# A gated linear attention and a spatial gating network on one core: weight loads on ScalarE's queue, with a new table of the order of all work

## The chip, the cores and the metric

One core of a Trainium2 chip. The metric is the device time of one execution in microseconds (us), lower is better. Engines: PE (TensorE, matmuls; PEld are its weight loads), DVE (VectorE), ACT (ScalarE), POOL (GpSimd), SP (SyncE, which here only requests DMA transfers).

## The reference

Two stages. The first is a recurrence over 768 time steps, for 4 batches and 8 heads of size 48; the second a network with a spatial gate on its result.

```python
# stage 1: q, k, v, alpha: (4, 8, 768, 48)
for t in range(S):
    state = alpha[:, :, t, :, None] * state + np.einsum('bhd,bhe->bhde', k[:, :, t], v[:, :, t])
    y[:, :, t] = np.einsum('bhd,bhde->bhe', q[:, :, t], state)
x = y.transpose(0, 2, 1, 3).reshape(B, S, H * D)             # (4, 768, 384)
# stage 2
h = np.maximum(x @ w_in, 0.0)                                # w_in (384, 1024)
u, v = h[..., :512], h[..., 512:]
v_n = (v - mean(v)) / np.sqrt(var(v) + 1e-06)                # over the last axis
v_s = np.einsum('ts,bsd->btd', w_spatial, v_n) + b_spatial   # w_spatial (768, 768)
return (u * v_s) @ w_out                                     # w_out (512, 384)
```

## The kernel before

The sequence is cut into chunks of 128 steps, six to a batch, 24 in all (numbered i). The recurrence within a chunk becomes matmuls with cumulative sums of log alpha. Chunks 0 to 7 are handled as four pairs (PAIRS, j = 0 to 3): one load of 384 KB per tensor brings 256 steps, two neighbouring steps to a partition, which are then split by parity (`par`). The other 16 chunks are loaded one by one (192 KB each).

**Steps of a pair** (function `pair`; the single chunks in `first` have the same ones without the final p): `lnp` takes the log of alpha on ACT (tile la); `cump` sums it with triangular matrices (le_pair, lt_pair) on PE; `einvp` and `eexpp` exponentiate on ACT; `ktp` and `qtp` scale k and q (tiles kt, qt; ktp on POOL or DVE, qtp on DVE); `vbp` casts v (POOL or ACT); `tr` transposes kt and qt on PE; `ev` copies the transposes out of PSUM (tile kqT, on ACT or DVE); `sc` forms scores on PE, and `m` masks them on DVE (tile ptm, masks mask2 and mask4); `updq` forms the chunk's contribution to the state; `z`, `S`, `sb` (DVE, POOL, POOL or DVE) bring the state forward and write it to the tile sbd; `ya` and `y` form the output on PE; `xs` copies it out, `xt` transposes it, `xe` copies it to xT.

**Steps of the second stage**, by batch b: `v.b.t` and `u.b.f.th` are the two halves of x @ w_in, evacuated with relu; `bn`, `rs`, `vn` normalise v; `s` multiplies by w_spatial (transposed once by `wt`, copied by `we`), and DVE adds the bias while it copies the result to a buffer vsb (the bias comes in by the matmuls `bb` and their copies `be` into bsp_bc); `g` multiplies by u (tile gT; POOL, in the last batch DVE too); `o` multiplies by w_out, and ACT copies the result out for the store `st`.

**Weights.** `fetch` loads six pieces of 768 KB: w_in in two halves (w_in.1 is for v, w_in.0 for u), w_spatial in three, w_out. A piece lands in one of two buffers raw_w and is cast from there (operations `cast`) to bf16 on POOL, ACT or DVE; a piece's request waits until the casts of the piece two before it are done. All requests, of q, k, v, alpha, of the weights and of the output's stores, are made by SP; only the small bias is requested by POOL.

**Order.** Nothing is scheduled when the kernel is built: each step is an `Op` with the engines that it may run on, and `PLAN` is a table written out in the code, which names every operation in the order of emission, with a letter for its engine (P, D, A, G for POOL, S for SP's request, Q for the landing). Each engine executes its operations in this order, and waits at each for its inputs. Numbers behind a colon are columns of filler: `bank` then first issues matmuls of the constant tile `junk` (128x128 fp32, set by a memset on DVE) on the bank that the operation is about to use. PE executes them whether or not the operation's inputs are there. Before has such fillers at ten places, 3,572 columns in all, 1,216 of them ahead of the first `cump`.

```python
for cols in fill:
    n = cols // 4
    nc.tensor.matmul(out=flat[:, 0:cols]..., lhsT=junk, rhs=junk[:, None, 0:n].to_broadcast([128, 4, n]), ...)
```

**Constants.** The operation `consts` emits memsets on DVE and triangles on POOL in one go, `junk` first; `cz` 0, 1 and 2 emit the rest (second buffers' padding, sbd, ones_row and eps; mask4 and ut_ones).

Of the kernel before, what the change touches and what calls it, by code (L numbers as in the profile page):

```python
# [36 lines left out]
class Slot:  # L37
# [5 lines left out]
    "kt": {"POOL": 0.9},  # L43
    "vb": {"POOL": 0.48, "ACT": 0.42},
# [6 lines left out]
    "o": {"ACT": 0.4},  # L51
# [6 lines left out]
S34 Q35 S36 Q37 G32 G0 Q33 S38 Q39 S94 Q95 S40 Q41 A42 P53:512:512:192 A54 D1 D2 D56 P43 S96 Q97 S98 Q99 S100 Q101  # L58
S163 Q164 S4 Q5 S165 Q166 S167 Q168 P59:464 G58 G48 A44 A45 A55 D46 D57 D47 P249:304 P49 P61 A50 P51 D52 D60 A62 A102
A250 P71:304 P74 P113 P103 D72 D73 D76 D75 P63 P77:172 D65 A114 D116 P119:148 A104 A64 A115 A105 A78 G66 G67 G106 D107  # L60
D117 D68 P79 P81 P111 P121 P247 P109 G3 G69 A108 A82 A80 D120 D122 D112 D110 P83 A84 A171 D248 S169 Q170 S9 Q10 S307
Q308 P131 P134 D133 D136 D132 D135 G70 G118 P172:228 P182 P123:240 A183 A8 A173 A124 P137 P138 A139 A174 G7 G6 D125
P85 G126 D128 D185 G127 G129 G175 P88 P142 P140 A86 A184 D176 D186 A143 A89 P188 P190 P180 P144 P178 A141 A191 A145
A181 P146 G11 G12 S309 Q310 S311 Q312 D130 D87 D179 D90 D189 P157 A187 A177 A158 A147 A13 P197 P200 P192 D199 D201
D198 D194 D202 P151:196 P155 A315 A193 A91 P326 P316 A327 P203 P153 P204 G195 G196 G329 A317 A328 A318 P149 A205 A154
D159 D156 D152 D330 G319 P208 P334 A209 P206 D320 P332 P324 P210 P322 D92 D335 D325 D333 D148 A207 P212 A211 A150 P347
P215 P221 A213 A160 A222 A216 S14 Q15 P223 P227 S18 Q19 D93 D323 D161 D348 D349 D214 G16 G17 A224 A228 P225 P229 A226
A21 P232 A234 D231 D230 D233 G20 P235:300 P238 S313 Q314 G331 G321 P344 P336 S367 Q368 S369 Q370 S22 Q23 S371 Q372
A237 A236 D217 D162 D346 A240 D338 A239 A218 D219 D220 A375 A337 P251 P263 P259 P376 A377 A378 G339 P264 D345 D341
D265 P260 D261 P255 P252 A380 A25 A24 D381 D253 P256 D257 G340 G342 G379 S409 Q410 S373 Q374 S446 Q447 S411 Q412 S413  # L70
Q414 S415 Q416 S26 Q27 S480 Q481 S448 Q449 S482 Q483 S450 Q451 S484 Q485 P383 A385 A417 S452 Q453 S577 Q578 S486 Q487
S581 Q582 S579 Q580 S583 Q584 P244 P241 P350 A246 D384 D245 D242 D243 P390 P354 P418 D392 D391 A351 A355 G262 G343
A420 A382 G254 G266 P279 P352 P271 P356 P393 P272 A353 A357 A419 G421 A422 A394 P280 P361 P386 P275 P395 A362 A424
A396 A31 D273 D423 D281 D387 P425 D397 D427 D426 D363 G282 G388 P276 P358 D277 P398 G258 G389 G278 G30 A399 A454 A359
A28 A488 P405 P432 P267 P455 P401 A402 A457 A456 D29 P291 P489 P268 A490 A459 D406 D433 D400 D434 D360 P283 P428 D269
D460 A492 D429 D493 G458 G491 P435 A284 A292 A436 G274 G461 G270 G430 G431 S648 Q649 S617 Q618 S650 Q651 S611 Q612
S652 Q653 S613 Q614 S690 Q691 S615 Q616 S694 Q695 S654 Q655 S692 Q693 P287 P462 P437 P495 P403 D463 D464 D497 D496
A288 A439 A438 P440 A585 A441 A364 D404 P469 P498 P295 P465 P586 P303 D471 D470 D466 D500 D499 A296 A587 A588 A590
A304 P299 G494 G467 G468 G589 G592 D591 D442 P472 A473 P501 P407 P474 A502 A300 P503 P593 P596 A443 A505 A408 D475
D476 P477 A478 D504 D366 D594 D595 D445 D444 D597 D365 P506 P600 P515 D601 D516 A507 A479 A508 D509 D602 A656 A510  # L80
A619 P517 P525 P513 P519 P529 P657 P533 P620 D511 D512 P526 P530 A514 A659 A658 A621 A661 A622 A698 A624 D518 D520
D527 D531 D662 P545 P534 P699 A701 A700 A703 D625 G598 G599 G660 G626 G623 G528 D535 P546 D547 P630 P627 P664 P537
# [12 lines left out]
D808 D906 D804 G805 G880 G809 G983 D985 D943 P822 P884 P811 D812 A885 P823 P908 P886 P945 D824 P814 P911 P815 D912
D909 D816 G813 G817 G913 G825 A910 A887 A888 A947 A946 P889 A1016 A890 P952 P915 P987 D953 D916 D954 P830 P1017 P831
P818 A988 A1019 A1050 A1018 D917 P948 P819 P1051 D949 A1021 A986 A989 D1022 D832 G950 P834 A1052 G951 G1020 P990 P842
P918 A835 A1054 D820 D991 D1055 A843 A919 P838 P1024 P994 P920 D1025 D921 D995 D996 A839 A1023 G914 G833 G1053 G992
S1048 Q1049 S575 Q576 S836 Q837 S844 Q845 S293 Q294 S289 Q290 S571 Q572 S305 Q306 S301 Q302 S555 Q556 A922 A1026 S297
Q298 S285 Q286 S840 Q841 P826 P955 P827 D828 A956 P1057 P957 P1031 D958 P1027 D1028 D1033 D1032 P997 P923 A1058 A1059  # L100
A959 P969 P1060 A1056 A998 P999 D1062 D1001 D1061 D970 G821 G829 G993 G1029 A1000 A924 P960 P846 P1034 A961 A847 G1030
P1063 A1035 A1064 P1002 P963 P1036 P1065 D925 D891 A1003 D962 D1066 P850 P967 A1067 A1037 D1004 A926 D928 P1068 A964
A1038 P1039 D927 D968 A851 A1005 A1069 A1040 D1006 D1041 D1007 D1070 P965 P854 P1076 P1080 P1078 P1074 D966 A1079 A855
A1071 A1081 D1075 D1072 D1073 D1077 P1094 P1082 P1106 P1086 P1083 P1098 P1095 P1090 P1102 P1087 P1107 P1091 P1103
P1110 P1099 P1111 D1096 D1084 G1085 D1088 D1097 D1108 D1092 D1093 G1089 P1113 D1104 G1109 G1105 D1112 D1100 D1101
P1117 P1121 S852 Q853 S563 Q564 S856 Q857 S848 Q849 A1114 S1115 Q1116 A1118 P1133 S1119 Q1120 A1122 P1125 A1134 S1123
Q1124 P1129 S1135 Q1136 A1126 P1137 S1127 Q1128 A1130 A1138 S1131 Q1132 S1139 Q1140
# [16 lines left out]
def kernel(  # L124
# [113 lines left out]
    def constants(_):  # L238

        nc.vector.memset(junk, 0.5)  # L240
        nc.gpsimd.memset(le_pair, 0.0)
        nc.vector.memset(mask2[:, 0].bitcast(FP32), 0.0)
        zero_padding(lap_bufs[0])
# [4 lines left out]
        nc.vector.memset(lt_pair.bitcast(FP32), 0.0)  # L248
        for t, base in ((le_pair, 0), (lt_pair, 1)):
            nc.gpsimd.affine_select(  # L250
                out=t, in_=t, compare_op=ALU.is_gt, fill=1.0, base=base, channel_multiplier=1,
                pattern=[[-1, 128]],
            )
            nc.gpsimd.memset(t[0:64, 64:128], 0.0)
        for t in (ktp_bufs[0], qtp_bufs[0]):
            zero_padding(t)
        make_identity(nc, ident)
        nc.vector.memset(mask2[:, 1].bitcast(FP32), 0.0)
        for par in range(2):
            for ci in range(2):  # L260
                rows = slice(64 * ci, 64 * ci + 64)
                nc.gpsimd.affine_select(
                    out=mask2[rows, par], in_=mask2[rows, par], compare_op=ALU.is_gt, fill=1.0,
                    base=par, channel_multiplier=2, pattern=[[0, 4], [-1, 2], [-2, 64]],
                )
# [891 lines left out]
```

## Time and profile before

| what | value |
|---|---|
| median of 3 runs | 143.13 us (143.12 to 143.7) |
| profiled execution, its own time | 143.08 us |
| its span in the profile | 141.3 us |
| clock granted to PE | 1.00 of full speed |
| DMA | 28.64 MB, mean 203 GB/s |
| first matmul of the second stage (v.0.0) | starts at 20.23 us |
| last matmuls end | about 138 us |

The span runs from the first to the last recorded activity; the time of an execution is 1.8 us longer. A line of the profile names the line of the code, the engine, the operation, the written tile, `<-` the read tiles, and the shape. In the views in order of time the first two columns are the start and the duration in us; in square brackets stands how long the engine had been idle and what ended that. Where several neighbouring instructions are merged, `x4` is their number. Durations of matmuls include some 0.17 us of a modelled tail, so the distance between two starts tells more than a duration. A request's line (SPq) shows how long the request held its engine, not the transfer.

### The profile page before, as it was taken

How to read it: one execution, taken by the hardware profiler on the slowest of the kernel's cores; microseconds unless marked ns; L12 is line 12 of the kernel's file. 1: busy time of each engine (PE TensorE's matmuls, PEld its weight loads, DVE VectorE, ACT ScalarE, POOL GpSimd, SP SyncE). 2: the span in 40 equal slices, each digit the busy share in tenths (PEclk: the TensorE clock that was granted, in tenths of full speed). 3: DMA queues.
4: the chain of work that ended last, by engine and by line, in shares of the span. 5: the costliest groups of instructions: out<-in, count | busy, mean ns of one | idle time of the engine just before them, and what ended most of it. 6: DMA issues, size and time to landing. Idle time of an engine off the chain costs nothing.

```text
span 141.3 us, 4968 instructions
## 1 busy us (share of the span) xinstructions
PE 133.2 (94%) x1912; PEld 84.2 (60%) x1923; DVE 118.3 (84%) x291; ACT 108.6 (77%) x282; POOL 83.4 (59%) x146
## 2 busy tenths in 40 slices
PE   7989798999999999999999999999999989999990
PEld 3457575575667656565675665656666656566560
DVE  7479878999989599999998898989979779894940
ACT  3677569988989969889887999997889969940061
POOL 6722986293449596982299899500799993000720
PEclk9999999999999999999999999999999999999999
DMA  4999999999898989989799999979978690112044
GB/s 102 323 323 332 331 272 311 225 320 238 241 232 156 283 161 208 205 161 212 154 205 179 193 217 177 222 143 195 250 151 203 225 375 24 70 56 102 0 164 170
DMA packets 89000, 28.64 MB, mean 203 GB/s; under 512 B 83728, under 2 KB 87440, under 8 KB 88976
## 3 DMA queue, kind: packets, MB, share of 16 engines
q1 hardware_dynamic: 88944, 28.32, 81.6%
q8 instruction: 15, 0.25, 0.7%
q14 instruction: 9, 0.07, 0.2%
q0 software_dynamic: 32, 0.00, 0.0%
HBM read 23.60 MB, written 4.72 MB: 200 GB/s over the span
## 4 chain that ended last, share of the span: by engine, by line
PE 71%; DVE 9%; POOL 7%; issue 5%; ACT 4%; ACTq 0%; POOLq 0%; DVEq 0%
PE bank L828 47%; PE bank L187 4%; DVE ptm L594 3%; PE bank L719 2%; PE bank L754 2%; POOL sbd L199 2%; POOL gT L989 2%; PE bank L511 2%; PE bank L782 2%; DVE ptm L765 2%; PE bank L740 1%; PE bank L583 1%; POOL kt L690 1%; PE bank L666 1%; DVE kqT L199 1%
## 5 line engine op out<-in xcount | busy, mean ns | idle before, releaser
L828 PE MATMUL bank<-w_spT,vn 128*128 128x384 bf16 x192 | 36.8, 326 | 0.0
L989 POOL TENSOR_TENSOR gT<-vsb,uT 128x384 bf16<-128x384 f32 x28 | 25.7, 923 | 14.9 <-DVE vsb L976 14.4
L690 POOL TENSOR_TENSOR kt<-kc,binv 128x384 bf16<-128x384 f32 x16 | 14.6, 914 | 13.4 <-ACT bc L685 8.6
L765 DVE TENSOR_TENSOR ptm<-bank,mask 128x512 bf16<-128x512 f32 x32 | 20.7, 682 | 1.9 <-PE bank L398 1.2
L828 PEld LDWEIGHTS <-vn 128*128 128x128 bf16 x192 | 16.6, 97 | 9.5 <-issue 0.2
L976 DVE TENSOR_TENSOR vsb<-bank,bsp_bc 128x384 f32<-128x384 f32 x31 | 16.5, 551 | 4.2 <-PE bank L828 2.5
L828 PE MATMUL bank<-xT,w_in 128*128 128x384 bf16 x96 | 18.7, 326 | 0.0
L828 PE MATMUL bank<-w_out_sb,gT 128*128 128x384 bf16 (+1 forms) x100 | 18.7, 319 | 0.0
L828 PE MATMUL bank<-w_in,xT 128*128 128x512 bf16 x61 | 17.2, 379 | 0.8 <-issue 0.2
L344 POOL TENSOR_TENSOR state<-state,bc 128x192 f32<-128x192 f32 x20 | 10.4, 520 | 11.4 <-DVE state L337 5.4
L197 ACT COPY kqT<-bank 128x512 bf16<-128x512 bf16 x21 | 12.1, 599 | 3.9 <-PE bank L719 1.1
L199 POOL CAST sbd<-state 64x192 bf16<-64x192 f32 x38 | 13.3, 350 | 2.0
L893 DVE BATCH_NORM_STATS2 stats<-v_sb 128x6 f32<-128x512 bf16 x20 | 13.7, 683 | 0.3 <-ACT v_sb L203 0.3
L203 ACT ACTIVATE v_sb<-bank 128x512 bf16<-128x512 f32 x20 | 11.8, 605 | 1.4 <-PE bank L828 1.3
L197 ACT CAST x_sb<-bank 128x384 bf16<-128x384 f32 x24 | 11.4, 490 | 1.5 <-PE bank L623 1.3
L828 PEld LDWEIGHTS <-w_in 128*128 128x128 bf16 x96 | 8.8, 97 | 5.9
L828 PEld LDWEIGHTS <-gT 128*128 128x128 bf16 x100 | 8.9, 97 | 5.6 <-DVE gT L989 0.4
L199 DVE COPY kqT<-bank 128x512 bf16<-128x512 bf16 x27 | 10.5, 416 | 1.9 <-PE bank L511 1.0
L187 PE MATMUL bank<-junk 128*128 128x512 f32 (+9 forms) x24 | 10.2, 529 | 1.1 <-DVE junk L240 1.1
L594 DVE TENSOR_TENSOR ptm<-bank,mask 128x512 bf16<-128x512 f32 x16 | 10.2, 683 | 0.5 <-PE bank L583 0.4
L197 ACT COPY xT<-bank 128x192 bf16<-128x192 bf16 (+1 forms) x26 | 9.4, 379 | 1.6 <-PE bank L398 1.1
L197 ACT COPY o_sb<-bank 128x384 f32<-128x384 f32 x9 | 4.4, 484 | 8.0 <-PE bank L828 8.0
(126 smaller groups left out, 284.0 us busy)
## 6 DMA issues: line engine op xcount, KB each, us to landing
ac<-in_alpha_dram SPq DMA_DIRECT2D x16, 192.0 KB, 4.1
kc<-in_k_dram SPq DMA_DIRECT2D x16, 192.0 KB, 4.8
qc<-in_q_dram SPq DMA_DIRECT2D x16, 192.0 KB, 4.1
vc<-in_v_dram SPq DMA_DIRECT2D x16, 192.0 KB, 3.8
raw_w<-in_moe_w_spatial_dram SPq DMA_DIRECT2D x3, 768.0 KB, 6.8
out_dram<-raw_w SPq DMA_DIRECT2D x11, 192.0 KB, 2.5
out_dram<-o_sb SPq DMA_DIRECT2D x9, 192.0 KB, 1.8
ac<-in_alpha_dram SPq DMA_DIRECT2D x4, 384.0 KB, 5.0
```

The source lines that it names most:

```text
L187: nc.tensor.matmul(out=flat[:, 0:cols].rearrange("p (a b) -> p a b", a=4), lhsT=junk, rhs=junk[:, None, 0:n].to_broadcast([128, 4, n]), st ...
L197: nc.scalar.copy(out=out, in_=in_)
L199: ENG[eng].tensor_copy(out=out, in_=in_)
L203: nc.scalar.activation(out=out, in_=in_, func=AF.Relu)
L344: ENG[eng].tensor_tensor(out=st["state"], in0=st["state"], in1=st["bc"][:, :, None].to_broadcast([128, HP, D]), op=ALU.mult)
L594: nc.vector.tensor_tensor(out=st[f"ptm{par}"][:, s], in0=st[f"pt{s}{par}"], in1=mask2[:, par], op=ALU.mult)
L690: ENG[eng].tensor_mul(out=k_blocks(kt3)[:, :, :, 0:D], in0=quad(st["kc"]), in1=st["binv"])
L765: nc.vector.tensor_tensor(out=st["ptm"][:, s], in0=st[f"pt{s}"], in1=mask4, op=ALU.mult)
L828: return lambda ps: nc.tensor.matmul(out=out(ps), lhsT=lhsT(), rhs=rhs(), start=start, stop=stop)
L893: nc.vector.bn_stats(out=stats, in_=d["v_sb"][:, tt, :])
L976: nc.vector.tensor_tensor(out=hold["vs"], in0=ps[:, 0:TH], in1=bsp_bc[:, th, :], op=ALU.add)
L989: ENG[eng].tensor_tensor(out=bt[b]["gT"][:, dsl, cols], in0=hold["vs"], in1=bt[b]["uT"][:, dsl, cols], op=ALU.mult)
```

## The change

Four things change.

1. The six weight pieces are requested by ACT on its own queue (`nc.scalar.dma_start`) in place of SP.
2. `PLAN` is replaced as a whole. PE has the same operations; the order on all engines, the engines of many operations, and the fillers are new: 6,060 columns at six places. 1,216 go ahead of the first bias matmul `bb` (now the first operation of PE, in front of `cump.0`), 916 ahead of `cump.1`, 1,260 and 1,024 ahead of the first transposes, 632 ahead of `tr.q.1.0`, 1,012 ahead of `updq.0`, and none later. SP now requests alpha of pairs 0 and 1 first, then k and q of both, then v of both.
3. The engines that some operations may use are widened: kt, vb, vbp, o, xs, and g in every batch may go to DVE too. By the tables this moves to DVE: 5 more g (8 in all, 3 before), 3 kt, 5 vb, 3 o, half of the last o, 4 xs, 8 xe, a bias copy and a cast of w_in; from DVE: 10 u and 8 ev to ACT, 2 ktp and one sb to POOL.
4. The constants are single operations (`c_junk`, `c_la`, `c_kt`, ...), each with its place in the table, and each step waits for those it reads. On DVE the order becomes la, ones_col, mask2[0], sbd, qt (second buffer), ones_row and eps, mask2[1], kt, la (second), halves_of with lt_pair, junk, qt, and further on the second kt. On POOL it becomes the bias request, one half of mask2, ident, the triangles, the other half of mask2.

Besides, the bias of the last `s` group is added by ident and bsp_bc in place of ones_row and b_sp_sb.

```diff
 ENGINES = {
-    "kt": {"POOL": 0.9},
-    "vb": {"POOL": 0.48, "ACT": 0.42},
+    "kt": {"POOL": 0.9, "DVE": 0.47},
+    "vb": {"POOL": 0.48, "ACT": 0.42, "DVE": 0.27},
...
-    "o": {"ACT": 0.4},
+    "o": {"ACT": 0.4, "DVE": 0.47},
...
 PLAN = """
-S34 Q35 S36 Q37 G32 G0 Q33 S38 Q39 S94 Q95 S40 Q41 A42 P53:512:512:192 A54 D1 D2 D56 P43 S96 Q97 S98 Q99 S100 Q101
...
+S49 Q50 D1 G47 Q48 D7 D15 S109 Q110 D11 G16 S51 Q52 D6 S53 Q54 D12 D17 D2 G9 D4 D13 D0 G14 D3 S113 Q114 A57
+P264:512:512:192 P262 D265 G18 P58 D5 S111 Q112 A117 P68 D263 A59 P128:512:404 A69 S55 Q56 P118 G61 A70 A60 G71
+P64:512:512:236 A119 S115 Q116 D62 A129 D72 P66:512:512 A120 P74 A130 P76 S178 Q179 D122 A67 D77 P126:512:120 A65 D132
...
-    op(("consts",), "POOL", 4.0, constants, prio=-10.0)
-    op(("cz", 0), "DVE", 1.7, zeros(0), prio=-5.0)
-    op(("cz", 1), "DVE", 0.7, zeros(1), prio=-4.0)
-    op(("cz", 2), "POOL", 1.2, zeros(2), [made[("consts",)]], prio=-3.0)
+    op(("c_junk",), "DVE", 0.17, lambda _: nc.vector.memset(junk, 0.5), prio=-20.0)
+    for n in range(2):
+        for x, us, t in (("la", 0.17, lap_bufs[n]), ("kt", 0.49, ktp_bufs[n]), ("qt", 0.17, qtp_bufs[n])):
+            op(("c_" + x, n), "DVE", us, lambda _, t=t: zero_padding(t), prio=-19.0 + 10 * n)
...
-            op(("g", b, dsl, th), {"POOL": 0.9} if b < B - 1 else {"POOL": 0.9, "DVE": 0.69}, None, gm, got(("s", b, dsl, th)), prio=Q)
+            op(("g", b, dsl, th), {"POOL": 0.9, "DVE": 0.47}, None, gm, got(("s", b, dsl, th)), prio=Q)
...
         def load(_):
             flat = raws.tile([128, n * cols], FP32, name="raw_w")
             hold["w"] = flat.rearrange("p (n f) -> p n f", n=n)
-            nc.sync.dma_start(out=hold["w"], in_=src)
-
-        dma(key, WT, load, list(fetched[-NRAW] if len(fetched) >= NRAW else []), prio, issue=0.68)
+            nc.scalar.dma_start(out=hold["w"], in_=src)
+
+        dma(key, WT, load, list(fetched[-NRAW] if len(fetched) >= NRAW else []), prio, "ACT", issue=0.43)
```

More of the change, by code (lines that the diff above doesn't have):

```diff
@@ L63 @@
[L63 to L82, printed above, removed]
@@ L236, in zero_padding, with triangle, c_col, c_ut @@
             nc.vector.memset(flat[:, :, 0::3, 0:D // 2], 0.0)
[L238 to L243, printed above, removed]
-        nc.vector.memset(ones_col, 1.0)
+    def triangle(t, pattern, base=0, step=1):
+        nc.gpsimd.affine_select(
+            out=t, in_=t, compare_op=ALU.is_gt, fill=1.0, base=base, channel_multiplier=step, pattern=pattern)
+    def c_col(_):
+        nc.vector.memset(ones_col, 1.0)
+    def c_ut(_):
+        nc.gpsimd.memset(ut_ones, 0.0)
+        triangle(ut_ones, [[-1, 128]])
+    def c_m4(_):
+        nc.gpsimd.memset(mask4.bitcast(FP32), 0.0)
+        triangle(mask4, [[0, 4], [-1, 128]])
+    def c_sbd(_):
+        for t in sbd_bufs:
+            nc.vector.memset(t.bitcast(FP32), 0.0)
+    def c_row(_):
+        nc.vector.memset(ones_row, 1.0)
+        nc.vector.memset(eps_tile, LN_EPS)
+    def c_half(_):
         nc.vector.memset(halves_of, 0.0)
@@ L248, in constants, with c_tri, c_m2, emit @@
         nc.vector.memset(lt_pair.bitcast(FP32), 0.0)
+    def c_tri(_):
+        nc.gpsimd.memset(le_pair, 0.0)
         for t, base in ((le_pair, 0), (lt_pair, 1)):
[L250 to L253, printed above, removed]
+            triangle(t, [[-1, 128]], base)
             nc.gpsimd.memset(t[0:64, 64:128], 0.0)
[L255 to L259, printed above, removed]
[L260 to L288 removed]
+    def c_m2(par):
+        def emit(_):
+            for ci in range(2):
+                triangle(mask2[64 * ci:64 * ci + 64, par], [[0, 4], [-1, 2], [-2, 64]], par, 2)
         return emit
@@ L365, in xs @@
             copy(eng, st["x_sb"], st["y"].rearrange("p h d -> p (h d)").rearrange("p (k t) -> p k t", k=KS))
-        op(("xs", i), "ACT", 0.38, xs, got(("y", i), ("xt", i - WK)), prio=P + 9, use=[st["sl_y"]])
+        op(("xs", i), {"ACT": 0.38, "DVE": 0.47}, None, xs, got(("y", i), ("xt", i - WK)), prio=P + 9, use=[st["sl_y"]])
         if i // 2 in PAIRS:
@@ L463, in cum @@
                         start=(p2 == 0), stop=(p2 == 1))
-            op(("cump", j, par), "PE", 0.33 + 0.1, cum, got(("lnp", j)), prio=P + 2, take=sl_c[par], cols=768)
+            op(("cump", j, par), "PE", 0.33 + 0.1, cum, got(("lnp", j), ("c_tri",)), prio=P + 2, take=sl_c[par], cols=768)
             def einv(_, par=par):
@@ L485, in ktf @@
                     in0=quad(st["kc"][:, :, par, :]), in1=quad(st[f"binv{par}"]))
-            op(("ktp", j, par), {"POOL": 0.9, "DVE": 0.6}, None, ktf, got(("einvp", j, par), ("kc", 2 * j), ("cz", 0)) + tr_users("k", jo), prio=P + 4)
+            op(("ktp", j, par), {"POOL": 0.9, "DVE": 0.6}, None, ktf, got(("einvp", j, par), ("kc", 2 * j), ("c_kt", j % NKP)) + tr_users("k", jo), prio=P + 4)
             def qtf(_, par=par):
@@ L492, in qtf @@
                     in1=quad(st[f"cum{par}"][:, 0:DM].rearrange("p (h d) -> p h d", h=H)))
-            op(("qtp", j, par), "DVE", 0.47, qtf, got(("eexpp", j, par), ("qc", 2 * j), ("cz", 0)) + tr_users("q", jo), prio=P + 4, use=[sl_c[par]])
+            op(("qtp", j, par), "DVE", 0.47, qtf, got(("eexpp", j, par), ("qc", 2 * j), ("c_qt", j % NKP)) + tr_users("q", jo), prio=P + 4, use=[sl_c[par]])
             def vbf(eng, par=par):
@@ L499, in vbf @@
                 copy(eng, st["vb"][:, par], st["vc"][:, :, par, :])
-            op(("vbp", j, par), {"POOL": 0.47, "ACT": 0.42}, None, vbf, got(("vc", 2 * j), ("y", 2 * j - 5), ("y", 2 * j - 6)), prio=P + 4.5)
+            op(("vbp", j, par), {"POOL": 0.47, "ACT": 0.42, "DVE": 0.27}, None, vbf, got(("vc", 2 * j), ("y", 2 * j - 5), ("y", 2 * j - 6)), prio=P + 4.5)
             for nm, bufs in (("k", ktp), ("q", qtp)):
@@ L563, in pair @@
         o = op(("updq", j), "PE", 0.5, upd,
-               got(("ktp", j, 0), ("ktp", j, 1), ("vbp", j, 0), ("vbp", j, 1)), prio=P + 7,
+               got(("ktp", j, 0), ("ktp", j, 1), ("vbp", j, 0), ("vbp", j, 1), ("c_half",)), prio=P + 7,
                take=[T[i]["sl_t"] for i in chunks], cols=768)
@@ L672, in first @@
         sl_c = Slot(ring)
-        op(("cum", i), "PE", 0.17 + (0.0 if last else 0.1), cum, cols=390, deps=got(("ln", i), ("trk", i - NB)), prio=P + 2, take=sl_c)
+        op(("cum", i), "PE", 0.17 + (0.0 if last else 0.1), cum, cols=390, deps=got(("ln", i), ("trk", i - NB), ("c_ut",), ("c_col",)), prio=P + 2, take=sl_c)
         def einv(_):
@@ L768, in first @@
         for s, sl in ((0, sl0), (1, sl1)):
-            op(("m", i, s), "DVE", 0.6, mk(s), got(("sc", i), ("y", i - WK), ("cz", 2)), prio=P + 7.5, use=[sl])
+            op(("m", i, s), "DVE", 0.6, mk(s), got(("sc", i), ("y", i - WK), ("c_m4",)), prio=P + 7.5, use=[sl])
         def y(_):
@@ L861, in bias @@
             sl = Slot(ring)
-            op(("bb", th), "PE", 0.2, emit, got(("b_sp",), ("cz", 1)), prio=50.0, take=sl)
+            op(("bb", th), "PE", 0.2, emit, got(("b_sp",), ("c_row",)), prio=50.0, take=sl)
             op(("be", th), {"DVE": 0.47, "ACT": 0.38}, None,
@@ L958, in second_s @@
             mms.append(mm(
-                lambda ps: ps[:, 0:TH], lambda: ones_row, lambda: b_sp_sb[:, th * TH:(th + 1) * TH], True, False))
+                lambda ps: ps[:, 0:TH], lambda: ident, lambda: bsp_bc[:, th, :], True, False))
         for st in range(NT):
@@ L980, in second_s @@
         pdeps = [[made[("vn", b, t)] for t in tt] for tt in ((0, 1, 2, 3), (4, 5))]
-        us = us + got(*[("we", 3 * th + t, r) for t in range(3) for r in range(2)])
+        us = us + got(*[("we", 3 * th + t, r) for t in range(3) for r in range(2)]) + (got(("be", th)) if last else [])
         group(("s", b, dsl, th), mms, 0.165, [made[("v", b, t)] for t in range(NT)] + us,
@@ L1056, in second_o @@
         made[("all", b)] = made.get(("o", b, tt))
-    op(("consts",), "POOL", 4.0, constants, prio=-10.0)
-    op(("cz", 0), "DVE", 1.7, zeros(0), prio=-5.0)
-    op(("cz", 1), "DVE", 0.7, zeros(1), prio=-4.0)
-    op(("cz", 2), "POOL", 1.2, zeros(2), [made[("consts",)]], prio=-3.0)
+    op(("c_junk",), "DVE", 0.17, lambda _: nc.vector.memset(junk, 0.5), prio=-20.0)
+    for n in range(2):
+        for x, us, t in (("la", 0.17, lap_bufs[n]), ("kt", 0.49, ktp_bufs[n]), ("qt", 0.17, qtp_bufs[n])):
+            op(("c_" + x, n), "DVE", us, lambda _, t=t: zero_padding(t), prio=-19.0 + 10 * n)
+    op(("c_col",), "DVE", 0.12, c_col, prio=-18.0)
+    op(("c_ut",), "POOL", 0.42, c_ut, prio=-20.0)
+    op(("c_id",), "POOL", 0.5, lambda _: make_identity(nc, ident), prio=-19.0)
+    op(("c_m4",), "POOL", 0.95, c_m4, prio=-8.0 if PAIRS else -18.0)
+    op(("c_sbd",), "DVE", 0.62, c_sbd, prio=-9.5)
+    op(("c_row",), "DVE", 0.22, c_row, prio=-9.4)
+    if PAIRS:
+        op(("c_half",), "DVE", 0.45, c_half, prio=-18.5)
+        op(("c_tri",), "POOL", 1.15, c_tri, got(("c_half",)), prio=-20.5)
+        for par in range(2):
+            op(("c_mz", par), "DVE", 0.25, lambda _, par=par: nc.vector.memset(mask2[:, par].bitcast(FP32), 0.0), prio=-18.2)
+            op(("c_m2", par), "POOL", 1.4, c_m2(par), got(("c_mz", par)), prio=-18.0 + par)
     pieces = [
```

116 lines of the change are left out of this document (57 added, 59 removed).

## The prediction

> **What bounds the kernel now.** I read the engine shares first, then the first 30 us in order of time, then the busy time by stretches of 5 us, and last the chain of waits. The shares:
>
> ```profile
> PE 133.2 (94%) x1912; PEld 84.2 (60%) x1923; DVE 118.3 (84%) x291; ACT 108.6 (77%) x282; POOL 83.4 (59%) x146
> ```
>
> Stretches of 5 us (columns: PE, PEld, DVE, ACT, POOL busy; clock, DMA share, GB/s), one at the start and two later:
>
> ```profile
> 5.00:10.00 5.00, 4.77 (x58) 2.64 (x58) 2.86 (x6) 3.35 (x8) 2.11 (x4) 1.00 1.17 324
> ...
> 50.00:55.00 5.00, 5.00 (x40) 2.70 (x39) 4.84 (x12) 3.78 (x10) 3.63 (x8) 1.00 0.89 176
> ...
> 65.00:70.00 5.00, 5.00 (x43) 2.88 (x42) 4.85 (x15) 4.71 (x15) 1.22 (x3) 1.00 0.89 175
> ```
>
> From about 20 us on PE is full: adding what PE lacks to 5.00 in the stretches from 20 to 135 us gives 2.2 us. DVE is almost as full (4.84, 4.85). So a microsecond lost before 20 us has nearly nowhere to be made good. The start, in order of time (start, us):
>
> ```profile
> 0.83 0.17 DVE L240 MEMSET junk<- 128x128 f32 x1 [0.83 <-PEq L1141]
> 1.00 0.27 DVE L242 MEMSET mask<- 128x256 f32 x1
> ...
> 3.47 0.63 DVE L275 MEMSET sbd<- 128x192 f32 x3
> ```
>
> ```profile
> 1.05 4.16 PE L187 MATMUL bank<-junk 128*128 128x512 f32 x6 [1.05 <-DVE junk L240]
> 5.14 0.65 PE L461 MATMUL bank<-la,le_pair 128*128 128x384 bf16 x3
> ...
> 5.79 0.94 PE L187 MATMUL bank<-junk 128*128 128x464 f32 x2
> ...
> 20.23 1.46 PE L828 MATMUL bank<-w_in,xT 128*128 128x512 bf16 x5
> ```
>
> DVE sets `junk` first of all, and PE begins its filler 0.05 us after. The 1,216 filler columns take 4.16 us (3.4 ns a column), and the first real matmul (`cump.0`) follows at once; la was ready at 5.08 (4.24 + 0.84). The first matmul of the second half of the network, `v.0.0`, runs at 20.23. I use it as the mark: the same PE work stands behind it in both tables.
>
> **Part A, the order of the constants: +2.6.** `junk` goes from first to eleventh on DVE, and the first instruction of PE waits for it. Ahead of it now stand, by the start-to-start distances of the same memsets above: la 0.11, ones_col 0.05, mask 0.25, three sbd 0.59, qt 0.16, ones_row and eps 0.17, mask 0.25, kt 0.47, la 0.16, halves_of with lt_pair 0.45: 2.66. The memset of junk (0.17) ends at 0.83 + 2.66 + 0.17 = 3.66 instead of 1.00. PE begins at 3.66 + 0.05 = 3.7, 2.6 later. Nothing covers this: PE is in order, and 1,216 columns of filler still come first.
>
> **Part B, from PE's start to v.0.0: +4.2.** Before, this took 20.23 - 1.05 = 19.2. Now: filler 4.16 (to 7.8); the two bias matmuls that went ahead, 0.4 (8.2); `cump.0` 0.65 (8.85). Here the filler is much longer: 916 + 1,260 + 1,024 + 632 + 1,012 = 4,844 columns stand between `cump.0` and `updq.0`, where before there were 464 + 304 + 304. A filler of 240 columns takes 0.40 and one of 464 about 0.77 (0.94 less 0.17 of modelled tail): 1.67 ns a column, so 8.1 us that PE must execute whether its data are there or not. Adding `cump.1` 0.65, four transposes of k and q 0.9, tr.q.1.0 0.2, two `sc` 0.5, three transposes 0.65 and `updq.0` 0.75 gives 8.85 + 8.1 + 3.65 = 20.6 for the end of `updq.0` (before: 12.1). From there the state update sets the pace: z.0 0.35 on DVE, m.1.0.0 and m.1.1.0 1.25 to 22.2; meanwhile S.0 and sb.0 on POOL 1.25, y.1, `cump.2`, xt.0, and `updq.1` ends at 24.2; z.1 0.35 and the last two m 1.25 (25.8); xs.1 and the cast of w_in.1 on DVE 1.0 (26.8); POOL has S.1, a cast, sb.1 and another cast (0.5, 0.6, 0.7, 0.6), ending at 27.0. So v.0.0 runs at 27.0: 23.4 after PE's start, 4.2 more than before. The loads are not what it waits for: the first is in at 4.24 and the fifth at 9.21 (where la and vbp stop waiting for them), 1.24 apart, so the eighth (vc.2) is in by 12.9. The triangles for `cump` come later on POOL too, behind one half of mask2 and ident (1.4 + 0.5 + 1.2 from 1.9): 5.0, hidden by the filler till 8.2; without that cover they would end with la at 5.1.
>
> **Part C, the weights on ACT: nothing on the path.** Six issues leave SP and enter ACT. Rows on SP:
>
> ```profile
> 9.02 1.11 SPq L441 DMA_DIRECT2D ac<-in_alpha_dram  x1
> 10.17 1.33 SPq L1081 DMA_DIRECT2D raw_w<-in_moe_w_in_dram  x1
> ...
> 18.22 0.42 SPq L441 DMA_DIRECT2D ac<-in_alpha_dram  x1
> ```
>
> With the queue full an issue holds its engine for 1.1 to 1.8, with it idle 0.42. ACT's own queue holds one piece at a time (two raw_w buffers), so I take 0.42: 6 x 0.42 = 2.5, bounds 2.5 and 6 x 1.8 = 10.8. ACT's list loses other work: ten u, eight ev to it (+9.7 by 494 and 599 ns), but xs, xe, vb, o, casts and be leave (-12.9): -0.7 with the issues. Behind each issue wait evacuations of banks that PE needs; w_in.1's stands ahead of ev.q.1.0, in the stretch in which PE runs filler. The request of w_in.1 moves from 10.17 to about 16.9 (behind ev.k.0.1); landing 7.1 later at 24.0 it is still ahead of its casts, from 25.1 on. SP's qc.6 waits for that landing too; before it was held till 24 as well (19.84 + 4.11). SP's list is otherwise the same loads and stores, but eight stores instead of two go ahead of the last loads: 6 x 192 KB at 324 GB/s, 3.6 us later for kc.23 and qc.22. Compute that is 6.8 later covers this; without that cover it costs up to 3.6.
> The Trainium skill (DMA: Bandwidth & Descriptors, section "Issuing engines are not separate DMA queues") says that issues from several engines run on the same 16 DMA engines, and save only the issuing sequencer's time. The trace agrees so far as it can (0.9 DMA share at 175 GB/s from one queue); by that rule this part gives nothing either.
>
> **Part D, engines after the mark: +1.85.** By counts of the two tables and mean durations DVE gets five gT (734 ns), three kt (570, as its pair form), five vb (350, as the cast of w_out_sb), eight xe (250), four xs and three o (550 each, as the cast of bsp_bc), one be, a cast and a half o (1.3): 14.3; it loses ten u (546), eight ev (416), two ktp (566) and one sb (0.67): 10.6. Net +3.7. POOL nets -2.0 (five gT and three kt of 0.92 go; two ktp, one sb, four casts come). With DVE at 92 to 97% in most stretches, +3.7 is the upper end; 0 is the lower, where DVE's own gaps take it. I take half. In the last `s` group one bias matmul through ident (326 ns) stands for one through ones_row (331): nothing. The gT row itself is uncertain:
>
> ```profile
> 130.39 3.00 POOL L989 TENSOR_TENSOR gT<-vsb,uT 128x384 bf16<-128x384 f32 x3 [12.51 <-DVE vsb L976]
> ```
>
> ```profile
> 131.20 0.55 DVE L989 TENSOR_TENSOR gT<-vsb,uT 128x384 bf16<-128x384 f32 x1
> ...
> 132.72 1.09 DVE L989 TENSOR_TENSOR gT<-vsb,uT 128x384 bf16<-128x384 f32 x1
> ```
>
> On DVE it took 0.55 or, beside POOL's gT, 1.09.
> The Trainium skill (SBUF — State Buffer, "Who interferes with whom") speaks against this part: a DVE instruction with two SBUF inputs blocks, or is blocked by, a GpSimd instruction that reads SBUF. The row of 1.09 agrees; if all eight gT met it, DVE would have 8 x 0.36 = 2.9 more than my mean counts, and the sum would be 1.4 higher.
>
> **Part E, slack and tail: -0.8.** Of the 2.2 us of PE's gaps after 20 us some wait for loads (w_in 1.1); with compute later, loads are ahead. Bounds 0 and -2.2; middle -1.1. The last operation is now a whole o (evacuation 0.48 for 0.32, store twice as large): +0.3.
>
> **Sum:** 2.6 + 4.2 + 0 + 1.85 - 0.8 = +7.85 on a span of 141.3, thus 149.15. The profiled run took 143.08, 1.8 more than its span, and the median is 143.13: 143.1 + 7.85 = 150.9.
>
> **Rivals.** (1) The lag is mostly made good. Before, between 20.45 and 25.89 the chain of waits leaves PE for 5.4 us (ACT, DVE: v_sb, qt, sbd, stats, kqT). If the late start hides that, and DVE's extra is hidden too: 143.1 + 6.8 - 5.4 + 0.3 = 144.8; with DVE's 1.85, 146.6. Against it: pair 2 still has the same steps. About 146, chance 0.20. (2) ACT and DVE become the bound: issues at the price of a full queue add 6 x (1.4 - 0.42) = 5.9 on ACT, gT at 1.09 2.9 on DVE; half of both on the path, on top of the sum: 155.3. For it: ACT is 4.9 of 5 busy at 85 to 95 us. Chance 0.17. (3) Faster: POOL decides. Twice the chain lies on POOL, 80.45 to 86.44 and 109.51 to 113.57 (10.1 us), with POOL at 4.7 to 4.8 of 5. If moving gT and kt off POOL removed both, the time is 143.1 + 6.8 - 10.1 + 0.3 = 140.1; it is faster once the relief exceeds 7.1. Against it: PE is still over 4.6 of 5 busy there, so there is little for it to gain. Chance 0.05; the same mechanism just cancelling the lag, 0.03.
>
> **Numbers.** Forecast (lag kept, 148 to 153) 0.55; rivals as above. A measurement of this kernel tells about 0.5% from no change. The range 145.5 to 154.5 takes the forecast, nearly all of rival 1 and half of rival 2. Faster 0.05, same 0.03, slower 0.92.
>
> **What would show it.** The first filler of PE at 3.7 behind the memset of junk; `cump.0` at 8.2; `updq.0` ending near 20.6; v.0.0 at 27; the six ACT issues at 0.4 each; DVE about 3 us busier; and after the mark as long to the end as before (117.8 us of PE). I am wrong if v.0.0 runs before 24, or if the stretch behind it is shorter by over 4 us.

## The result

| | before | after |
|---|---|---|
| median | 143.41 us (143.12 to 144.26, 4 runs) | 148.56 us (148.01 to 148.92, 4 runs) |
| ratio to before | 1 | 1.0345, 95% interval 1.0287 to 1.0404 |
| span of the profiled execution | 141.3 us | 146.6 us |
| v.0.0 begins, in the profile | 20.23 us | 26.12 us |

The change makes the kernel 5.15 us slower. It was forecast at 150.9 (145.5 to 154.5): slower, by the lag of the start, but by 7.85 and not 5.15. Medians here are over all executions of a kernel, and ratios over those within 1.5% of its fastest; outside of that lie one each of e2, e4 and e6, two of e5 (the profiled one among them) and six of the twelve of e10, and there the two figures differ.

The engine shares of after:

```profile
PE 136.0 (93%) x1913; PEld 85.2 (58%) x1927; DVE 123.1 (84%) x300; ACT 106.9 (73%) x273; POOL 82.5 (56%) x146
```

PE is busy 2.8 us longer and DVE 4.8, where 3.7 was forecast at most. Stretches of 5 us in after (columns as before: PE, PEld, DVE, ACT, POOL busy; clock, DMA share, GB/s):

```profile
5.00:10.00 5.00, 5.00 (x13) 2.00 (x13) 1.44 (x4) 1.61 (x3) 1.56 (x4) 1.00 1.17 324
50.00:55.00 5.00, 4.84 (x74) 3.40 (x70) 4.74 (x11) 4.06 (x11) 4.13 (x8) 1.00 0.95 191
65.00:70.00 5.00, 4.94 (x84) 3.31 (x84) 4.97 (x14) 4.47 (x14) 2.43 (x6) 1.00 0.99 194
```

From 5 to 10 us PE executes 13 instructions where before it executed 58, and is called full: that is filler. Later the stretches are about as full as before's (4.84 and 4.94 of 5 for 5.00). The start of after, PE in order of time behind DVE's memset:

```profile
3.45 0.17 DVE L1050 MEMSET junk<- 128x128 f32 x1
```

```profile
3.67 4.42 PE L188 MATMUL bank<-junk 128*128 128x512 f32 x6 [3.67 <-DVE junk L1050]
8.02 0.74 PE L848 MATMUL bank<-b_sp_sb,ones_row 1*128 1x384 bf16 x2
8.70 0.34 PE L452 MATMUL bank<-la,le_pair 128*128 128x384 bf16 x1
...
9.36 1.70 PE L188 MATMUL bank<-junk 128*128 128x512 f32 x4
...
21.05 0.57 PE L544 MATMUL bank<-vbp,kt 64*128 64x48 bf16 x32
...
26.12 0.38 PE L819 MATMUL bank<-w_in,xT 128*128 128x512 bf16 x1
```

PE starts 2.62 late, at 3.67, and v.0.0 comes at 26.12, 5.89 late (the row at 21.05 is `updq.0`, used further below). From there on no more is lost, and 0.6 us are gained by the end. On DVE, the first mask of chunk 8 and the last gT (before, then after):

```profile
45.00 1.28 DVE L765 TENSOR_TENSOR ptm<-bank,mask 128x512 bf16<-128x512 f32 x2
...
135.24 0.56 DVE L989 TENSOR_TENSOR gT<-vsb,uT 128x384 bf16<-128x384 f32 x1
```

```profile
50.96 1.27 DVE L756 TENSOR_TENSOR ptm<-bank,mask 128x512 bf16<-128x512 f32 x2
...
140.56 0.55 DVE L980 TENSOR_TENSOR gT<-vsb,uT 128x384 bf16<-128x384 f32 x1
```

The mask is 5.96 late and the last gT 5.32: between them lie 90.24 us before and 89.60 after.

### The profile page after: what moved, and what is told of

It reads as the page before. It is cut to its first block, busy times and chain, and to the rows that moved or that the text cites. A ratio compares the mean times of both kernels' runs of the same rounds, so it can differ in the third digit from the quotient of the medians.

```text
span 146.6 us, 4961 instructions
## 1 busy us (share of the span) xinstructions
PE 136.0 (93%) x1913; PEld 85.2 (58%) x1927; DVE 123.1 (84%) x300; ACT 106.9 (73%) x273; POOL 82.5 (56%) x146
## 4 chain that ended last, share of the span: by engine, by line
PE 67%; DVE 16%; ACT 7%; issue 3%; DMA 2%; POOL 2%; POOLq 0%; DVEq 0%
PE bank L819 39%; PE bank L188 9%; DVE ptm L585 3%; PE bank L745 3%; PE bank L710 2%; DMA ac<-in_alpha_dram 2%; PE bank L502 2%; DVE qt L691 2%; PE bank L773 2%; PE bank L731 2%; PE bank L767 2%; DVE vb L200 1%; DVE vn L916 1%; PE bank L389 1%; POOL w_in L200 1%
## 5 line engine op out<-in xcount | busy, mean ns | idle before, releaser
L819 PE MATMUL bank<-w_spT,vn 128*128 128x384 bf16 x192 | 35.7, 326 | 0.0
L980 POOL TENSOR_TENSOR gT<-vsb,uT 128x384 bf16<-128x384 f32 x23 | 21.1, 930 | 18.7 <-DVE vsb L967 18.5
L198 ACT COPY kqT<-bank 128x512 bf16<-128x512 bf16 x29 | 16.0, 593 | 6.1 <-PE bank L502 3.2
L819 PE MATMUL bank<-xT,w_in 128*128 128x384 bf16 x96 | 19.7, 326 | 0.1
L681 POOL TENSOR_TENSOR kt<-kc,binv 128x384 bf16<-128x384 f32 x13 | 11.9, 924 | 9.4 <-ACT bc L676 8.5
L188 PE MATMUL bank<-junk 128*128 128x512 f32 (+5 forms) x28 | 13.5, 619 | 3.7 <-DVE junk L1050 3.7
L198 ACT CAST x_sb<-bank 128x384 bf16<-128x384 f32 x20 | 9.5, 487 | 5.2 <-PE bank L773 4.6
L204 ACT ACTIVATE uT<-bank 128x384 bf16<-128x384 f32 x24 | 11.3, 498 | 1.2 <-PE bank L819 1.2
L188 PEld LDWEIGHTS bank<-junk 128*128 128x128 f32 x28 | 5.7, 219 | 8.7 <-issue 4.9
L916 DVE TENSOR_SCALAR vn<-v_sb,mvs,rstd 128x512 bf16<-128x512 bf16 x24 | 10.4, 463 | 0.5 <-ACT rstd L909 0.5
```

What stands on the lines that cost most here:

```text
L188: nc.tensor.matmul(out=flat[:, 0:cols].rearrange("p (a b) -> p a b", a=4), lhsT=junk, rhs=junk[:, None, 0:n].to_broadcast([128, 4, n]), st ...
L198: nc.scalar.copy(out=out, in_=in_)
L204: nc.scalar.activation(out=out, in_=in_, func=AF.Relu)
L681: ENG[eng].tensor_mul(out=k_blocks(kt3)[:, :, :, 0:D], in0=quad(st["kc"]), in1=st["binv"])
L819: return lambda ps: nc.tensor.matmul(out=out(ps), lhsT=lhsT(), rhs=rhs(), start=start, stop=stop)
L916: nc.vector.tensor_scalar(out=d["vn"][:, t, :], in0=d["v_sb"][:, t, :], scalar1=d["mvs"][:, t, 0:1], scalar2=d["rstd"][:, t:t + 1], op0=AL ...
```

## The experiments

Four kernels first, to see which part of the start makes the loss.

**e1: junk first.** The memset of junk goes back to the head of DVE's list in the kernel after.

```diff
-S49 Q50 D1 G47 ... G9 D4 D13 D0 G14
+D0 S49 Q50 D1 G47 ... G9 D4 D13 G14
```

> The changed kernel with one move: the memset of junk is again the first on DVE. Theory (the start's delay is carried to the end): PE's filler runs from 1.05 to 5.4, cump.0 starts near 6.0 instead of 8.7, everything to v.0.0 comes 2.6 to 2.8 earlier, span 144.0 and time 145.8. Rival (the delay is taken up by waits for data before v.0.0, and the loss comes from the engines' new loads): v.0.0 stays at 26 and the time within 0.7 of 148.6.

Measured: 149.03 us, ratio 1.0398 (1.0337 to 1.0458), as slow as after, although the start was mended: PE's filler began at 1.05 and v.0.0 at 23.12, 3.0 us earlier. The gain was gone again by chunk 8's mask, at 51.28 (after: 50.96). ACT in that stretch of e1 (start, us, line, operation; in brackets the idle time before it and what ended it):

```profile
42.62 0.47 ACT L686 ACTIVATE bank<-bank 128x384 f32<-128x384 f32 x1
45.95 0.38 ACTq L1084 DMA_DIRECT2D raw_w<-in_moe_w_out_dram  x1
46.38 0.18 ACT L550 ACTIVATE bc<-bank 128x8 f32<-128x8 f32 x1 [3.28 <-DMA ac<-in_alpha_dram]
```

ACT's queue has reached the request of w_out at 43.1, and stands. What lets it go is no weight: it is a load of alpha that SP requested. The chain of waits of e1 has the same piece:

```profile
40.02 5.83 DMA ac<-in_alpha_dram
...
45.95 0.38 ACTq L1084
46.33 0.05 issue
46.38 0.14 ACT bc L550
```

In the program as it is built the requests of both queues share eight landing counters (semaphores), given out in turn, and an engine that comes to a request first waits until the transfer that used its counter last has landed. For w_out in e1 that is the alpha of chunk 13, which the view above has from 40.02 to 45.85. While the request stands, ACT executes none of the evacuations behind it. That made a new theory, tested in e6.

**e2: no filler.** The five later fillers of after are removed; the first (1,216 columns) stays.

```diff
-P128:512:404 ... P64:512:512:236 ... P66:512:512 ... P126:512:120 ... P78:512:500
+P128 ... P64 ... P66 ... P126 ... P78
```

> The changed kernel without its five later fillers (4,844 columns); the first, 1,216, and the late memset of junk stay. Theory (PE executes filler while data are there): updq.0 ends near 15 instead of 21.6, v.0.0 runs at 21 to 22, time 144. Rival 1 (the data come no earlier, filler only covers waiting): v.0.0 at 26, time 148.5. Rival 2 (without filler PE's clock falls): the transposes and scores before v.0.0 take twice as long each, and the time is above 146.

Measured: 147.15 us, 1.0224 (1.0147 to 1.0301), from 145.57 to 149.13; v.0.0 at 22.94, 3.2 earlier than in after, and not at 21 to 22. The first theory's 144 us was missed; the second rival fits better: the granted clock was 0.76 from 16 to 23 us. **e3: both**, junk first and no later filler (the two diffs together).

> Both: junk first on DVE, and no filler but the first. Theory: the start is then bound by loads, updq.0 by vc.0 (lands at 11.2) near 13, v.0.0 at 19 to 20 by the landing and the casts of w_in.1; time 141.5 to 143, level with the kernel before or better. Rival (the new table is also worse behind v.0.0): v.0.0 at 19 to 20, but the time stays above 145.

Measured: 144.83 us, 1.0103 (1.0069 to 1.0137); v.0.0 at 20.63, 0.4 behind before's. The forecast of 141.5 to 143 was missed: from v.0.0 to the last gT e3 takes 116.34 us and before 115.01, so 1.3 us go behind the mark, where the granted clock was still 0.74 from 20 to 25 us; that the clock is all of it is not shown. Ahead of the mark too PE slowed down where the filler had been. Stretch 16 to 23 us of e3, and matmuls in it:

```profile
16.00:23.00 7.00, 6.42 (x97) 4.32 (x98) 3.97 (x9) 4.82 (x11) 5.32 (x11) 0.53 1.04 294
```

```profile
16.73 1.12 PE L452 MATMUL bank<-la,le_pair 128*128 128x384 bf16 x3 [0.36 <-ACT la L443]
17.65 0.52 PE L452 MATMUL bank<-la,lt_pair 128*128 128x384 bf16 x1
```

The granted clock is 0.53, and `cump` takes 1.12 and 0.52 where after has 0.65 and 0.33. The filler is not only waste: it holds the clock. None of PE's gaps in e3 between 5 and 16 us was longer than 0.78.

**e4: weights on SP.** The table of after with the six requests on SP again, at the same places.

```diff
-            nc.scalar.dma_start(out=hold["w"], in_=src)
+            nc.sync.dma_start(out=hold["w"], in_=src)
```

> The changed kernel and its table with the six weight requests given back to SP, at the same places of the table. Theory (the queue matters for nothing on the path): 148.6 within 1.0; the six issues take 1.0 to 1.8 each on SP instead of 0.4 on ACT. Rival (requests on ACT's queue delay its evacuations, or their pieces collide with SP's loads): faster than 147.5. Second rival (the second queue helps): slower than 149.6.

Measured: 151.12 us, 1.0504 (1.0434 to 1.0575). With this table the second queue is worth 2.6 us by the medians and about 2.3 by the ratios. SP's waits in e4 (waited for, us in total, times, longest):

```profile
SPq L1084 <- POOL w_in L200: 4.9, 2, 3.7
SPq L1084 <- POOL w_row L200: 4.3, 1, 4.3
```

L1084 is the weights' request: on SP it stands 9.2 us for a free raw_w buffer, with the chunk loads behind it; the DMA share in e4 from 35 to 40 us is 0.64 (after: 1.15). The chain of waits fits: loads of q and alpha make 11.3% of it in e4, and a load of alpha 2.4% in after. That the stands make the late loads is read from these rows, no run tests it by itself.

Four more, to separate the start from the stand.

**e5: the second queue alone.** The kernel before, with its own table, and only the weights' requests on ACT.

```diff
-S4 Q5 ... S9 Q10 ... S14 Q15 ... S18 Q19 ... S22 Q23 ... S26 Q27
+A102 A4 Q5 ... A171 A9 Q10 ... A145 A14 Q15 ... A315 A18 Q19 ... G17 A22 Q23 ... A385 A26 Q27
```

> The kernel before with its own order, fillers and constants; only the six weight requests go from SP's queue to ScalarE's, each at the place in ScalarE's order whose work ran at the moment SP made that request in the profile of before (10.2, 17.0, 24.1, 27.2, 34.1 and 44.1 us). This is the change's title alone. Theory Q (the second queue costs nothing, the loss is made by the new order's start): 142 to 144 us, ScalarE's issues 0.4 us each, last weight landing by 51 us. Rival H (a request on ScalarE stands until the transfer that last used its landing counter is in, and holds ScalarE's engine meanwhile): 144.5 to 148 us, with idle times of ScalarE of 1 us or more ahead of a request, put down to a landing.

Measured: 145.11 us, 1.0099 (1.0064 to 1.0134). Its request of w_out stood as in e1, this time for a load of k:

```profile
44.52 0.58 ACT L197 COPY kqT<-bank 128x512 bf16<-128x512 bf16 x1 [0.33 <-PE bank L719]
48.12 0.42 ACTq L1081 DMA_DIRECT2D raw_w<-in_moe_w_out_dram  x1
48.59 0.52 ACT L660 ACTIVATE la<-ac 128x384 bf16<-128x384 f32 x1 [3.49 <-DMA kc<-in_k_dram]
```

PE in that profile waited 3.3 us for this la. The profiled execution was the longest of the eight, 148.98 us, so its stand can't be taken as the size in the others. By the time the rival held (144.5 to 148).

**e6: e1 with w_out's request four instructions later**, where its counter was last used by ACT's own w_sp.2.

```diff
-A395 D235 P274 A41 Q42 S495 ... A352 A40 ... A254 ... A255
+A395 D235 P274 S495 ... A352 A40 ... A254 ... A255 A41 Q42
```

> As e1_junk_first (the kernel after with the memset of junk first on VectorE), and the request of w_out four instructions later in ScalarE's order, behind the second of the two w_spT evacuations that follow it, where the built order gives it a landing counter that only ScalarE's own earlier weight piece used. In e1 that request stood for 3.3 us until SP's load of ac had landed (ScalarE idle from 43.1 to 46.4 us). Theory H (that stand ate e1's earlier start): ScalarE's idle time there is gone, m.8.0 comes 2.5 to 3 us earlier than e1's 51.9, and the time falls from 149.0 to 145.5 to 146.8. Rival D (VectorE's backlog of 31 to 42 us or the late w_in.0 ate it): 148.3 to 149.5.

Measured: 146.15 us, 1.0204 (1.0154 to 1.0254): 2.9 less than e1, as the stand predicted, and 2.4 less than after. ACT in e6:

```profile
41.86 0.47 ACT L686 ACTIVATE bank<-bank 128x384 f32<-128x384 f32 x1
42.07 0.37 ACTq L1084 DMA_DIRECT2D raw_w<-in_moe_w_out_dram  x1
42.25 0.17 ACT L550 ACTIVATE bc<-bank 128x8 f32<-128x8 f32 x1
```

The idle time is gone, and chunk 8's mask comes at 48.30, against 51.28 in e1.

**e7: before with junk's memset late**, behind DVE's other constants; the padding of the second buffers, which came next in `zeros`, now stands ahead of it, and no other memset moves by more than 0.15 us.

```diff
-        nc.vector.memset(junk, 0.5)
         nc.gpsimd.memset(le_pair, 0.0)
...
+        for t in (lap_bufs[1], ktp_bufs[1], qtp_bufs[1]):
+            zero_padding(t)
+        nc.vector.memset(junk, 0.5)
```

> The kernel before with one change: the memset of junk stands behind VectorE's other constants (3.5 us) as in the kernel after, not first (0.8 us), so that TensorE's first filler starts about 2.6 us later, with the old order, the old fillers and the old queue behind it. Theory S (TensorE has no slack behind its start, so a late start is carried to the end): 145.5 to 146.5 us. Rival (the waits ahead of 60 us give it back): 143.2 to 144.3.

Measured: 146.12 us, 1.0177 (1.0141 to 1.0213): 2.7 us for a start that is 2.49 later:

```profile
3.54 3.94 PE L187 MATMUL bank<-junk 128*128 128x512 f32 x6 [3.54 <-DVE junk L267]
```

A late first filler costs its whole lateness in the old table.

**e8: e6 with w_in.0 requested about 3 us earlier** in ACT's list, behind the first ebcp.

```diff
-A95 A24 Q25 ... A139
+A79 A24 Q25 ... A95 ... A139
```

> As e6_junk_wout, and the request of w_in.0 about 3 us earlier in ScalarE's order (behind the first ebcp, near 18.8 us, in place of 21.8). Theory W (TensorE's waits between 25 and 31 us in e1 are for the casts of w_in.0, which landed at 29.0): the piece lands near 25, v.0.0 to v.0.3 come without a wait for POOL, and 0.8 to 1.5 us less than e6. Rival (the transfer only lengthens, since two queues already fill the DMA engines there, and the loads of chunks 4 and 6 come later): e6's time within 0.5 us, or more.

Measured: 147.57 us, 1.0286 (1.0242 to 1.0329). Inconclusive: in its profiled execution PE's clock rose later than in e6's. The same rows in e6 and then e8:

```profile
1.05 3.96 PE L188 MATMUL bank<-junk 128*128 128x512 f32 x6 [1.05 <-DVE junk L1050]
...
6.31 1.70 PE L188 MATMUL bank<-junk 128*128 128x512 f32 x4
```

```profile
1.05 4.42 PE L188 MATMUL bank<-junk 128*128 128x512 f32 x6 [1.05 <-DVE junk L1050]
...
7.42 3.23 PE L188 MATMUL bank<-junk 128*128 128x512 f32 x4
```

The second filler takes 1.70 in one and 3.23 in the other, and the matmuls behind it begin at 7.85 in e6 and at 10.47 in e8, ahead of anything that the move of w_in.0 touches. These 2.62 are all of the lag of v.0.0 (25.70 for 23.07). From v.0.0 to the last gT e8 takes 114.64 and e6 115.08, 0.4 less where 0.8 to 1.5 was expected. The six times themselves (146.46 to 148.43) lie above four of e6's six; how many of them began as slowly is not recorded, so what the earlier request is worth stays open.

Two last, to see whether the parts add up.

**e9: e5 with w_out's request earlier** (behind ebcp.3), where its counter is ACT's own.

```diff
-A337 ... A385 A26 Q27
+A337 A26 Q27 ... A385
```

> As e5_before_act_queue (the kernel before with all six weight requests on ScalarE), and the request of w_out earlier in ScalarE's order, behind ebcp.3 (about 41 us), where the landing counter that it gets was last used by ScalarE's own w_sp.2 (in by 39.7 us); in e5 it stood from 45.1 to 48.1 us until SP's load of kc for chunk 11 had landed. Theory H (that stand is what the second queue cost in the old order): no idle time of ScalarE of over 1 us ahead of that request, and 142.5 to 143.8 us, the time of before or a little less. Rival (the queue costs by the other requests too, or by weights that take the DMA engines from the chunk loads): 144.3 to 145.5, as e5.

Measured: 144.11 us, 1.0055 (1.0035 to 1.0075), 1.0 less than e5 by the medians and 0.6 by the ratios. The request goes without a stand (41.72, with ACT idle 0.79 ahead of its next instruction, for POOL). It lies between the two expectations: without the stand the second queue brings nothing in the old order, and e9 is 0.6 us above before by the medians. In its profile most of that is made at the start, before any weight is requested: PE's first real matmuls, `cump.0`, took 1.17 and not 0.65, as the clock rose later.

```profile
5.27 1.17 PE L461 MATMUL bank<-la,le_pair 128*128 128x384 bf16 x3
```

v.0.0 begins 0.70 behind before's (20.93), and from there to the last gT e9 takes 115.35 for 115.01. So at most the other 0.34 can be the queue's in this execution; for the rest of the seven it is not settled.

**e10: e6's idea with short fillers.** Junk first, the five later fillers cut to 304, 304, 304, 172 and 304 columns, w_out's request where its counter is long free. The five had 4,844 columns and now have 1,388; the 3,628 in the expectation below is a slip.

```diff
-P128:512:404 ... P64:512:512:236 ... P66:512:512 ... P126:512:120 ... P78:512:500
+P128:304 ... P64:304 ... P66:304 ... P126:172 ... P78:304
```

> The kernel after with junk's memset first, the five later fillers cut from 3,628 columns to 1,388 (304, 304, 304, 172, 304), and the request of w_out behind the second w_spT evacuation ahead of its place, where its counter was last used by the load of vc for chunk 8 (in by 38 us). Theory B (what is left of the loss behind e6 is the fillers' length, and short ones hold the clock as in the kernel before): v.0.0 at 20.5 to 21.5 us, no matmul of 384 columns at 0.53 us behind 12 us, and 143.3 to 144.5 us. Rival (short fillers let the clock fall as in e3_both, or the new order loses it elsewhere): 144.8 to 146 us.

Measured: 1.0053 (1.002 to 1.0086) over the six shorter executions; the median of all 12 is 145.44, 2.0 above before's and in the rival's range, and they spread from 143.25 to 147.03, where before's eighteen spread by 1.1. In the profiled one, the shortest, of 143.25, v.0.0 comes at 19.84, ahead of before's:

```profile
13.11 0.34 PE L536 MATMUL bank<-halves_of,la 128*128 128x2 bf16 x8
...
17.49 0.65 PE L452 MATMUL bank<-la,le_pair 128*128 128x384 bf16 x3 [1.19 <-ACT la L443]
...
19.84 1.46 PE L819 MATMUL bank<-w_in,xT 128*128 128x512 bf16 x5
```

`cump` takes 0.65 there, full speed, behind a gap of 1.19; with no later filler (e3) v.0.0 came 0.79 later. In other executions of e10 the mean clock was down to 0.975 or 0.988, so fillers this short don't hold it each time; but two of 145.67 and 146.40 us had a mean of 1.00, so the mean clock doesn't explain all of the spread. At its best, with the start mended and the fillers short, the new order with the second queue is level with before but for 0.5%; in half of the executions it is not. None of the versions beats before.

## Why the prediction was right, step by step

**Part A, the constants: right.** +2.6 was said, PE's first filler is 2.62 later, and e7 shows that this alone costs 2.7 us. e1 seemed to refute it; e6, 2.4 us below after, shows that e1's earlier start was eaten by a stand which it brought about itself: in the program built from the other order w_out's request draws another counter. In after that counter was last used by the load of kc for chunk 9, and ACT was idle for only 0.55 there.

**Part B, PE's start to v.0.0: right in kind, 0.9 too large, by two errors that partly cancel.** Forecast +4.2 (23.4 for 19.2), measured 26.12 - 3.67 = 22.45, +3.3. The filler was priced well: from start to start the five later ones took 8.3 us, for 8.1. But `cump.0` began at 8.70 and not 8.2, and `updq.0` ended at 21.6 and not 20.6, 1.0 late; and from there to v.0.0 it took 4.5 us where the working, with the state update setting the pace, had 6.4. So the total came closer than its two halves, which is luck. That the fillers are the cause, e10 and e6 show, which both start PE at 1.05: with 1,388 later columns for 4,844, v.0.0 comes at 19.84 for 23.07, 3.2 us earlier. The 3,456 columns less are 5.8 us at the prediction's 1.67 ns, so 2.6 of them do not come back: PE's first real matmuls began 0.40 later in e10 (6.05 for 5.65), and then it waits for data, 0.35 for qt and 1.19 for la, at full clock. With no later filler at all the clock falls as well, to 0.53 in e3. The working took filler as pure cost, and names neither.

**Part C, the weights on ACT: nothing on the path, right here, and by luck.** The issues took 0.38 to 0.43 each, as said. Two things were missed. The queue is worth about 2.3 us under this table (e4), most likely because SP no longer stands for a raw_w buffer. And its price is not the issue but the stand on a shared counter: 3.3 us in e1, 3.5 in e5's profile. The other direction shows in after itself, SP's waits:

```profile
SPq L432 <- DMA raw_w<-in_moe_w_in_dram: 5.6, 1, 5.6
SPq L637 <- DMA raw_w<-in_moe_w_in_dram: 5.6, 1, 5.6
```

SP stood twice for ACT's weights to land, 5.6 us each, one of which the prediction named (qc.6). The loads behind them came in time for PE: from 5 to 53 us its waits in after sum to 1.7 us, and none names a load. The rule of the Trainium skill that the prediction quoted, from DMA: Bandwidth & Descriptors, section "Issuing engines are not separate DMA queues", that issuing from another engine saves only the issuing sequencer's time, agrees with e9 (nothing gained). It is too small for e4, where the sequencer's time included 9.2 us of waiting for buffers.

**Part D, engines behind the mark: the term that failed.** +1.85 was taken, between 0 and 3.7. DVE did get 4.8 us more, with slower single instructions than their nearest rows, as here in after (count | busy us, mean ns | idle before):

```profile
L916 DVE TENSOR_SCALAR vn<-v_sb,mvs,rstd 128x512 bf16<-128x512 bf16 x24 | 10.4, 463 | 0.5 <-ACT rstd L909 0.5
L980 DVE TENSOR_TENSOR gT<-vsb,uT 128x384 bf16<-128x384 f32 x8 | 5.2, 659 | 0.1
L200 DVE CAST vb<-vc 128x384 bf16<-128x384 f32 x5 | 3.5, 693 | 0.0
```

The cast of vb was priced at 350 and took 693; vn went from 402 to 463. Yet none of it came out at the end: from v.0.0 to the last gT after takes 114.44 and before 115.01. The lower bound was the right one. That PE and not DVE sets the pace there is read from the chain of waits (67% of after's lies on PE, 16% on DVE; before, 71% and 9%); no run takes the moves between engines back by themselves. The rule on DVE and GpSimd sharing SBUF (the Trainium skill, SBUF — State Buffer, "Who interferes with whom") fits the eight gT less than the single row of 1.09 did: their mean is 659 (541 to 1,002), below the 734 that was used. That DVE is slower beside POOL shows more clearly in the casts of vb, which have one input: one took 0.36 at 73.20, while POOL executed nothing, and two took 0.97 and 1.07 at 88.11 and 105.22, beside POOL's kt. The price of 350 came from a single cast.

**Part E, slack and tail:** -0.8 was taken; parts D and E together should have given +1.05 and gave -0.6 from v.0.0 to the last gT.

**The sum:** 2.6 + 3.3 - 0.6 is 5.3, the difference of the spans (146.6 - 141.3). Against 7.85 the excess is 0.9 in part B and 1.65 in D and E. Rival 1, the lag made good, did not come about; of rival 2 only DVE's longer instructions came about, off the path; rival 3 had the sign wrong.

## What to carry to other kernels

An instruction that starts PE late costs its whole lateness when PE has no gaps behind it (e7: 2.7 us for 2.49); so look first at what the first matmul waits for. When a second engine gets a DMA queue, look up which landing counter each of its requests takes and who used it last: the request may stand for the other queue's transfer, with that engine's compute behind it. And filler beyond what PE would have waited anyway is paid for (3.2 of 5.8 us in e10), but taking all of it away lets the clock fall (e3): its length is to be tried on the chip, and judged by several executions.

## What the runs showed of the hardware

- PE runs slowly at first, both when it starts early and when it starts late: the first 1,216 columns of filler took 4.16 us from 1.05 in before and 4.42 from 3.67 in after (3.4 and 3.6 ns a column), the next 916 in after 1.70 (1.9, with the modelled tail). The Trainium skill (TensorE: Matmul & The Clock Gate, "What's actually happening") gives about 3.4 us of activity until the clock is doubled, varying from run to run. The traces here show more, and not one figure: in before full speed is there at 5.14, 4.1 us behind PE's start, in e9 at 6.55, 5.5 behind it; in e8 the filler still took twice its time from 7.42 on, until 10.47, 9.4 us behind PE's start. The granted clock in the profile reads 1.00 in all these stretches; only the durations tell.
- Without later filler the granted clock fell to 0.53 (e3, 16 to 23 us), though no gap of PE from 5 to 16 us was longer than 0.78; in the profiled execution of e10, with 1,388 columns of later filler, it did not, even behind a gap of 1.19 us.
- On DVE, a cast of 128x384 from fp32 took 350 ns once in before; in after the five of vb took 360 to 1,066, shortest with POOL idle and longest beside POOL's kt.
